# One core, infini-attention with a gated MLP: the prologue, the memory update and the down projection in another order

## The chip, the core and the metric

The kernel runs on one core of a Trainium2 chip. Five engines run their own instruction streams in order and wait for each other through semaphores: TensorE (PE: matmuls and transposes; its weight loads are listed as PEld), VectorE (DVE), ScalarE (ACT), GpSimd (POOL) and SyncE (SP, which here only issues DMAs). The metric is the device time of one execution in microseconds; the lower the better.

## The reference, cut to what matters

One transformer block on x of 2048 x 448 (16 heads of 28), whose two halves are modulated by a vector c. `silu(c) @ w_mod` gives six vectors of 448 (sa, ca, ga, sb, cb, gb).

```
h = layernorm(x) * (1 + ca) + sa
x = x + ga * attention(h)            # 4 segments of 512 rows
h = layernorm(x) * (1 + cb) + sb
x = x + gb * ((sigmoid(h @ w_gate) * (h @ w_up)) @ w_down)
```

In the attention each segment s has a causal softmax of its own (512 x 512 per head). From the second segment on its output is mixed, per head by sigmoid(beta), with a memory read phi(q) @ M / (phi(q) @ z + 1e-6), where M and z sum phi(k)^T v and phi(k) over the segments before. phi(t) is t + 1 for t > 0 and exp(t) below.

## The kernel before, in words

Everything stays on chip: x is loaded as 16 tiles of 128 rows, four to a segment, and the weights are loaded once.

**Steps of a segment s.** `ln1(s)` (L201) normalises four tiles with `ln_tile` (L179): statistics on DVE (`st` L182, `mv` L183), then on POOL the variance plus epsilon (`ve` L185) and its power -0.5 (`rs` L187), then the normalised tile `xn` on DVE (L189). `proj_jobs(s)` transposes them on PE in four chunks (`lntr` L195), which DVE scales into `hT` (L196); then come, for four head groups hc of four heads each, the q and k projections (`pq` L220, cast by ACT into `qT` and by DVE into `kT`), and four v projections (`pv` L231, cast by ACT into `vt`). `mem_jobs(s)` makes phi(k): PE transposes kT (`ptk` L243), ACT takes exp (`ek` L245, two buffers), POOL clips it (L246), DVE adds (`pk` L247); then PE makes the memory's update (`dM` L257), which DVE adds into M and POOL masks into `rm`. Per head group there are three `logits` calls g = 0, 1, 2 (`lg` L290, one PSUM tile of four banks, exp by ACT L293, causal mask by POOL L296), `pv` (`acc` L309 and, for s > 0, the memory read `mem` L316, normalised by DVE and added by POOL into `ou` L343) and `otr` (L351, transposed output to `oT`). `wo_jobs(s)` projects, adds x and runs the second layernorm of each tile on its own (`wo_tile` L354 to L364). `h2_jobs(s)` transposes again, `gu_jobs(s)` makes 14 gate and up tiles (`gps` L373, tanh by ACT L375, `ups` L378, product by DVE into `fT` L381), `down_jobs(s)` four tiles of 14 matmuls each (`dps` L386, residual by DVE L390, stored by SP).

**Modulation.** `mod_cols` (L156) makes sa, ca, sb and cb as columns; `prep_b1` folds ga into w_o on POOL (L438, 4 products) and `prep_b3` folds gb into w_down on POOL (L447, 14 products).

**Order.** PE runs in the order of the calls (`manual_schedule`); for the other engines and queues the framework's scheduler sets the order. PSUM has four one-bank tiles for everything but the logits; a tile is given out when an earlier one's reader is done. The main loop (L469 to L495) calls `logits` for each s, hc and g and between them takes jobs from a list `fill` until a quota of nanoseconds, estimated in the code, is used up. w_q and w_k come in through a staging area in `wd_sb` and are spread by ACT (L101) and POOL (L102). w_down is loaded there later.

## Time and profile before

| | |
|---|---|
| median of 3 runs | 350.73 us (349.46 to 351.97) |
| the profiled execution | 349.13 us |
| its span, first to last instruction | 347.4 us |
| mean granted TensorE clock | 0.916 of full speed |
| busy share of the span | PE 80%, DVE 49%, ACT 41%, POOL 34% |

The span and the chain of waits belong to one profiled execution, which was 1.6 us under the median. In the profile a busy time is the sum of an engine's instructions. The idle time before an instruction is put down to what released it. The granted clock is given as a share of 2.4 GHz, so 0.50 is 1.2 GHz. In the timeline, rows are runs of like instructions: start, time from the first start to the last end, engine, line, operation, output and input, count, and in brackets the idle time before.

### The profile page before, as it was taken

The page shows a single profiled execution, that of the slowest core. Times are in us where ns is not written, and L with a number is a line of the kernel's source. Part 1 is how long each engine was busy: PE and PEld are TensorE (multiplying, and loading weights), DVE is VectorE, ACT ScalarE, POOL GpSimd, SP SyncE. Part 2 cuts the span into 40 slices and gives each one's busy share as a digit, 9 for nine tenths or more (in the row PEclk, how much of TensorE's full clock was granted, in tenths as well). Part 3 has the DMA queues.
Part 4 walks back from the last instruction along what each step waited for, and adds up shares of the span by engine and source line. Part 5 has one row for each costly group of instructions (what it writes and reads, how often), then busy time and mean ns, then how long its engine had stood idle before and what let it go on. Part 6 is the DMA issues. An engine that isn't in the chain of part 4 may idle for free.

```text
span 347.4 us, 5518 instructions
## 1 busy us (share of the span) xinstructions
PE 277.8 (80%) x2232; PEld 144.5 (42%) x2232; DVE 171.0 (49%) x382; ACT 142.0 (41%) x169; POOL 119.3 (34%) x209
## 2 busy tenths in 40 slices
...
GB/s 179 296 288 308 69 2 0 47 48 0 2 2 0 0 2 0 3 0 2 28 26 0 2 0 2 0 29 27 2 1 2 0 2 32 23 1 0 2 13 40
DMA packets 12473, 12.85 MB, mean 37 GB/s; under 512 B 1184, under 2 KB 11552, under 8 KB 12448
## 3 DMA queue, kind: packets, MB, share of 16 engines
...
## 4 chain that ended last, share of the span: by engine, by line
PE 61%; POOL 16%; DVE 10%; ACT 7%; DMA 3%; issue 2%; SPq 0%; POOLq 0%; ACTq 0%
PE gps L373 13%; PE dps L386 12%; PE ups L378 11%; PE pq L220 7%; PE acc L309 4%; POOL wd_sb L447 4%; POOL pT L296 3%; POOL rs L187 3%; PE lg L290 3%; ACT pT L293 3%; DMA wd_sb<-in_A_wq_dram 3%; PE lntr L195 2%; POOL ou L343 2%; DVE st L182 2%; DVE xn L189 2%; PE pv L231 2%
## 5 line engine op out<-in xcount | busy, mean ns | idle before, releaser
L293 ACT ACTIVATE pT<-lg 128x2048 bf16<-128x2048 f32 (+1 forms) x48 | 76.5, 1594 | 50.6 <-PE lg L290 48.2
L296 POOL TENSOR_SCALAR_AFFINE_SELECT pT<-pT 128x512 bf16<-128x512 bf16 x64 | 40.5, 646 | 100.8 <-ACT pT L293 100.7
L375 ACT ACTIVATE tt<-gps 128x512 f32<-128x512 f32 x56 | 33.3, 596 | 88.2 <-PE gps L373 86.8
L381 DVE SCALAR_TENSOR_TENSOR fT<-tt,ups 128x512 bf16<-128x512 f32 x56 | 38.5, 688 | 61.6 <-PE ups L378 36.9
L373 PE MATMUL gps<-hT,wg_sb 112*128 112x512 bf16 x224 | 60.5, 392 | 0.9 <-DVE hT L196 0.8
L378 PE MATMUL ups<-hT,wu_sb 112*128 112x512 bf16 x224 | 58.6, 385 | 0.0
L386 PE MATMUL dps<-wd_sb,fT 128*128 128x448 bf16 x224 | 43.9, 353 | 0.0
L195 PE MATMUL lntr<-ident,xn 128*112 128x128 bf16 x128 | 17.1, 299 | 23.0 <-DVE xn L189 22.3
L378 PEld LDWEIGHTS <-wu_sb 112*128 112x128 bf16 x224 | 22.2, 99 | 27.7 <-issue 2.2
L373 PEld LDWEIGHTS <-wg_sb 112*128 112x128 bf16 x224 | 20.2, 101 | 23.9 <-issue 6.3
L386 PEld LDWEIGHTS <-fT 128*128 128x128 bf16 x224 | 21.4, 98 | 19.7 <-issue 0.5
L195 PEld LDWEIGHTS <-xn 128*112 128x112 bf16 x128 | 13.5, 192 | 27.2 <-DVE xn L189 24.8
L390 DVE TENSOR_TENSOR ot<-dps,x_sb 128x448 bf16<-128x448 f32 x16 | 10.0, 624 | 28.0 <-PE dps L386 28.0
L220 PE MATMUL pq<-hT,wq_sb 112*128 112x512 bf16 x64 | 19.6, 422 | 2.8 <-DVE hT L196 2.6
L257 PE MATMUL dM<-vt,pk 128*128 128x116 bf16 x48 | 6.7, 293 | 18.8 <-DVE pk L247 18.8
L182 DVE BATCH_NORM_STATS2 st<-x_sb 128x6 f32<-128x448 bf16 x32 | 18.7, 608 | 5.1 <-DMA x_sb<-in_A_x_dram 4.9
L189 DVE TENSOR_SCALAR xn<-x_sb,mv,rs 128x448 bf16<-128x448 bf16 x32 | 13.3, 431 | 15.2 <-POOL rs L187 15.0
L309 PEld LDWEIGHTS <-pT 128*128 128x128 bf16 x640 | 18.7, 98 | 2.7 <-issue 0.4
L309 PE MATMUL acc<-vt,pT 128*128 128x29 bf16 x640 | 19.0, 178 | 0.0
L187 POOL TENSOR_TENSOR rs<-ve,mhalf 128x1 f32<-128x1 f32 x32 | 18.0, 569 | 1.7
L290 PE MATMUL lg<-qT,kT 28*128 28x512 bf16 (+3 forms) x256 | 17.7, 309 | 0.8 <-DVE kT L225 0.8
L220 PE MATMUL pq<-hT,wk_sb 112*128 112x512 bf16 x64 | 18.2, 410 | 0.0
...
## 6 DMA issues: line engine op xcount, KB each, us to landing
...
```

The lines of the kernel that those rows point to most:

```text
L187: nc.gpsimd.tensor_tensor(rs[:], ve[:], mhalf[:], ALU.pow)
L195: nc.tensor.transpose(pt[0:KP, t * P:(t + 1) * P], xns[t][:, kc * KP:(kc + 1) * KP], ident[:])
L220: nc.tensor.matmul(pq[:, 0:L], lhsT=head_cols(w_sb, k, hc), rhs=h[:, k, :], start=(k == 0), stop=(k == NK - 1))
L290: nc.tensor.matmul(lg[:, hs, wid:wid + nq], lhsT=kT[r, hc, kb * P:(kb + 1) * P], rhs=qT[r, hc, kb * P:L], start=True, stop=True, tile_posi ...
L293: nc.scalar.activation(pT[:, :, w0:w0 + wid], lg[:, :, 0:wid], AF.Exp, scale=scale)
L296: nc.gpsimd.affine_select(out=blk, in_=blk, compare_op=ALU.is_ge, fill=0.0, base=0, pattern=[[0, 4], [1, P]], channel_multiplier=-1)
L309: nc.tensor.matmul(accv[:, qb, hs, 0:ME], lhsT=pT[:, hs, c0:c0 + P], rhs=vt[:, kb, hc * 4 + hs, 0:ME], start=(kb == 0), stop=(kb == qb))
L373: nc.tensor.matmul(gp[:, 0:L], lhsT=wg_sb[:, k, fs], rhs=h[:, k, :], start=(k == 0), stop=(k == NK - 1))
L375: nc.scalar.activation(tt[:], gp[:, 0:L], AF.Tanh, scale=0.5)
L378: nc.tensor.matmul(up[:, 0:L], lhsT=wu_sb[:, k, fs], rhs=h[:, k, :], start=(k == 0), stop=(k == NK - 1))
L381: nc.vector.scalar_tensor_tensor(ft[:], tt[:], 1.0, up[:, 0:L], op0=ALU.add, op1=ALU.mult)
L386: nc.tensor.matmul(dp[:, 0:D], lhsT=fT_of[(s, fc)][:, t * P:(t + 1) * P], rhs=wd_sb[:, fc, :], start=(fc == 0), stop=(fc == NFC - 1))
```

## The change

Nothing is computed differently but for one thing: the power -0.5 of the first layernorm is taken for the four tiles of a segment in one POOL operation of 128 x 4 instead of four of 128 x 1. The second layernorm still goes tile by tile. All else is order:

- The first layernorm of segment 0 is emitted ahead of the spreading of w_q and w_k. The masks `bmask`, the gate `coef` and the ones in `vt` come after the first projections, in `late_consts`. Most loads come in `late_loads`, in another order.
- The four `mem_k` steps and the `dM` step stand between pieces of the next segment's projections instead of in a row. For segment 2 they stand inside segment 3's projections, behind `prep_b3`.
- In the main loop `pv` stands before `logits` of g = 1, each g has one quota instead of two halves, segments 1 to 3 share one quota that is worked out once, and the down projection of segment s-2 and the second layernorm's transposes are only put into `fill` after `wo_jobs(s-1)`, so the down projection stands between `wo_jobs` and those transposes.
- The tail has other limits: the quota leaves the time of six gate and up tiles unspent, and half of the down projection of segment 2 stands behind the last `wo_jobs`.

```diff
--- before.py
+++ after.py
@@ -89,52 +89,44 @@
     wm = {0: load_wm(nc.sync, 0), 1: load_wm(nc.scalar, 1)}
...
-    for k in range(NK):
-        nc.scalar.copy(wq_sb[:, k, :, 0:Dh], wq_st[:, k, :, :])
-        nc.gpsimd.tensor_copy(wk_sb[:, k, :, 0:Dh], wk_st[:, k, :, :])
     nc.sync.dma_start(wv_sb[:], A_wv.rearrange("(k p) n -> p k n", p=KP))
-    beta_t = const.tile([P, H], BF16)
-    nc.sync.dma_start(beta_t[:], A_beta.partition_broadcast(P))
-    for s in range(1, NSEG):
-        load_x(nc.sync, s * TPS, (s + 1) * TPS)
-    wm[2] = load_wm(nc.sync, 2)
-    wo_sb = wts.tile([KP, NK, D], BF16)
-    nc.sync.dma_start(wo_sb[:], A_wo.rearrange("(k p) n -> p k n", p=KP))
-    wm[3] = load_wm(nc.sync, 3)
-    wm[4] = load_wm(nc.sync, 4)
-    wg_sb = wts.tile([KP, NK, F], BF16)
-    wu_sb = wts.tile([KP, NK, F], BF16)
-    for w_sb, w_dram in ((wg_sb, B_w_gate), (wu_sb, B_w_up)):
-        wv_ = w_dram.rearrange("(k p) n -> p k n", p=KP)
-        nc.sync.dma_start(w_sb[:, 0:2, :], wv_[:, 0:2, :])
-        nc.sync.dma_start(w_sb[:, 2:4, :], wv_[:, 2:4, :])
-    wm[5] = load_wm(nc.sync, 5)
-    nc.sync.dma_start(wd_sb[:], B_w_down.rearrange("(fc p) n -> p fc n", p=P))
+
+    def late_loads():
+        load_x(nc.sync, TPS, 2 * TPS)
+        nc.sync.dma_start(beta_t[:], A_beta.partition_broadcast(P))
+        wm[2] = load_wm(nc.sync, 2)
+        load_x(nc.sync, 2 * TPS, 3 * TPS)
+        nc.sync.dma_start(wo_sb[:], A_wo.rearrange("(k p) n -> p k n", p=KP))
+        wm[3] = load_wm(nc.sync, 3)
+        load_x(nc.sync, 3 * TPS, 4 * TPS)
+        for w_sb, w_dram in ((wg_sb, B_w_gate), (wu_sb, B_w_up)):
+            wv_ = w_dram.rearrange("(k p) n -> p k n", p=KP)
+            nc.sync.dma_start(w_sb[:, 0:2, :], wv_[:, 0:2, :])
+            nc.sync.dma_start(w_sb[:, 2:4, :], wv_[:, 2:4, :])
+        wm[4] = load_wm(nc.sync, 4)
+        nc.sync.dma_start(wd_sb[:], B_w_down.rearrange("(fc p) n -> p fc n", p=P))
+        wm[5] = load_wm(nc.sync, 5)
 
 
...
-    mhalf = const.tile([P, 1], F32)
+    mhalf = const.tile([P, TPS], F32)
     nc.gpsimd.memset(mhalf[:], -0.5)
-
     bmask = const.tile([P, NHC, 4, ME], BF16)
...
-    nc.scalar.activation(coef[:, 1, :], beta_t[:], AF.Tanh, scale=0.5)
-    nc.vector.tensor_scalar(coef[:, 1, :], coef[:, 1, :], 0.5, 0.5, op0=ALU.mult, op1=ALU.add)
-    nc.vector.tensor_scalar(coef[:, 0, :], coef[:, 1, :], -1.0, 1.0, op0=ALU.mult, op1=ALU.add)
-
     vt_all = [const.tile([P, TPS, H, HP], BF16, name=f"vt{s}") for s in range(NSEG)]
-    for s in range(NSEG):
-        nc.gpsimd.memset(vt_all[s][:, :, :, Dh:Dh + 1], 1.0)
+    def late_consts():
+        for s in range(NSEG):
+            nc.gpsimd.memset(vt_all[s][:, :, :, Dh:Dh + 1], 1.0)
+        nc.scalar.activation(coef[:, 1, :], beta_t[:], AF.Tanh, scale=0.5)
+        nc.vector.tensor_scalar(coef[:, 1, :], coef[:, 1, :], 0.5, 0.5, op0=ALU.mult, op1=ALU.add)
+        nc.vector.tensor_scalar(coef[:, 0, :], coef[:, 1, :], -1.0, 1.0, op0=ALU.mult, op1=ALU.add)
+
+        nc.gpsimd.memset(bmask[:], 1.0)
...
 
     def mod_cols(j, vi, plus_one):
         cp = m_f32("cp")
@@ -176,18 +176,21 @@
         return rep
 
 
-    def ln_tile(src):
-        st = work.tile([P, nc.vector.BN_STATS_DIM], F32, tag="st", bufs=4)
-        mv = work.tile([P, nc.vector.BN_AGGR_DIM], F32, tag="mv", bufs=4)
-        nc.vector.bn_stats(st[:], src)
-        nc.vector.bn_aggr(mv[:], st[:])
-        ve = work.tile([P, 1], F32, tag="ve", bufs=4)
-        nc.gpsimd.tensor_scalar(ve[:], mv[:, 1:2], EPS, None, op0=ALU.add)
-        rs = work.tile([P, 1], F32, tag="rs", bufs=4)
-        nc.gpsimd.tensor_tensor(rs[:], ve[:], mhalf[:], ALU.pow)
-        xn = work.tile([P, D], BF16, tag="xn", bufs=8, name="xn")
-        nc.vector.tensor_scalar(xn[:], src, mv[:, 0:1], rs[:, 0:1], op0=ALU.subtract, op1=ALU.mult)
-        return xn
+    def ln_tiles(srcs, key):
+        n = len(srcs)
+        mv = work.tile([P, n, nc.vector.BN_AGGR_DIM], F32, tag=f"mv{n}", bufs=3)
+        for i, src in enumerate(srcs):
+            st = work.tile([P, nc.vector.BN_STATS_DIM], F32, tag="st", bufs=4)
+            nc.vector.bn_stats(st[:], src)
+            nc.vector.bn_aggr(mv[:, i, :], st[:])
+        rs = work.tile([P, n], F32, tag=f"rs{n}", bufs=3)
+        nc.gpsimd.tensor_scalar(rs[:], mv[:, :, 1], EPS, None, op0=ALU.add)
+        nc.gpsimd.tensor_tensor(rs[:], rs[:], mhalf[:, 0:n], ALU.pow)
+        out = xns_of.setdefault(key, [])
+        for i, src in enumerate(srcs):
+            xn = work.tile([P, D], BF16, tag="xn", bufs=8, name="xn")
+            nc.vector.tensor_scalar(xn[:], src, mv[:, i, 0:1], rs[:, i:i + 1], op0=ALU.subtract, op1=ALU.mult)
+            out.append(xn)
 
     def h_chunk(xns, hT, kc, vi):
         pt = m_bf16("lntr")
@@ -199,7 +202,7 @@
     xns_of, hT_of = {}, {}
 
     def ln1(s):
-        xns_of[s] = [ln_tile(x_sb[:, s * TPS + t, :]) for t in range(TPS)]
+        ln_tiles([x_sb[:, s * TPS + t, :] for t in range(TPS)], s)
 
     def new_hT(key):
         hT_of[key] = pipe.tile([KP, NK, L], BF16, tag="hT", bufs=3, name="hT")
@@ -359,9 +362,7 @@
                              start=(k == 0), stop=(k == NK - 1))
         xt = x_sb[:, s * TPS + t, :]
         nc.vector.tensor_tensor(xt, pw[:, 0:D], xt, ALU.add)
-        if t == 0:
-            xns_of[("2", s)] = []
-        xns_of[("2", s)].append(ln_tile(xt))
+        ln_tiles([xt], ("2", s))
 
     fT_of = {}
 
@@ -448,64 +449,72 @@
 
 
     ln1(0)
+    for k in range(NK):
+        nc.scalar.copy(wq_sb[:, k, :, 0:Dh], wq_st[:, k, :, :])
+        nc.gpsimd.tensor_copy(wk_sb[:, k, :, 0:Dh], wk_st[:, k, :, :])
     mod_cols(0, 0, False)
     mod_cols(1, 1, True)
-    ln1(1)
+    late_loads()
     j0 = proj_jobs(0)
     for _, fn in j0[:7]:
         fn()
+    late_consts()
+    ln1(1)
+    j1, j2, j3 = proj_jobs(1), proj_jobs(2), proj_jobs(3)
+    m = [mem_jobs(s) for s in range(3)]
     fill.extend(j0[7:])
-    fill.extend(mem_jobs(0))
-    fill.extend(proj_jobs(1))
+    fill.extend(j1[:5] + m[0][0:2] + j1[5:7] + m[0][2:4] + j1[7:9] + m[0][4:] + j1[9:])
+    fill.append((0, lambda: ln1(2)))
     fill.append((1000, prep_b1))
-    fill.extend(mem_jobs(1))
-    fill.append((0, lambda: ln1(2)))
+    fill.extend(j2[:5] + m[1][0:2] + j2[5:7] + m[1][2:4] + j2[7:9])
     fill.append((2000, prep_b2))
-    fill.extend(proj_jobs(2))
     fill.append((0, lambda: ln1(3)))
+    fill.extend(m[1][4:] + j2[9:])
     fill.append((1000, prep_b3))
-    p3 = proj_jobs(3)
+    rest = j3[:5] + m[2][0:2] + j3[5:7] + m[2][2:4] + j3[7:9] + m[2][4:] + j3[9:]
+
+    def cost(jobs):
+        return sum(cst for cst, _ in jobs)
+
+    quota0 = cost(fill) / 12.0
+    tail_cover = 6 * 8 * MM
+    total = cost(rest) + sum(cost(wo_jobs(s) + h2_jobs(s) + gu_jobs(s)) for s in range(3)) \
+        + sum(cost(down_jobs(s)) for s in range(2)) - tail_cover
+    quota1 = total / 36.0
 
     for s in range(NSEG):
+        quota = quota0 if s == 0 else quota1
         if s == 1:
-            fill.extend(p3)
-            fill.extend(mem_jobs(2))
-        if s >= 2:
-            fill.extend(down_jobs(s - 2))
-        if s >= 1:
-            late = h2_jobs(s - 1) + gu_jobs(s - 1)
-        else:
-            late = []
-        total = sum(cst for cst, _ in list(fill) + late) + (wo_jobs(0)[0][0] * 4 if s else 0)
-        quota = total / 12.0
+            fill.extend(rest)
         debt = 0.0
         for hc in range(NHC):
+            prev = (s, hc - 1) if hc else (s - 1, NHC - 1)
             for g in range(3):
-                logits(s, hc, g)
-                prev = (s, hc - 1) if hc else (s - 1, NHC - 1)
-                debt = run_fill(quota / 2 + debt)
                 if prev[0] >= 0 and g == 1:
                     pv(*prev)
+                logits(s, hc, g)
+                debt = run_fill(quota + debt)
                 if prev[0] >= 0 and g == 2:
                     otr(*prev)
-                    if prev[1] == NHC - 1:
-                        fill.extendleft(reversed(wo_jobs(prev[0])))
-                        fill.extend(late)
-                debt = run_fill(quota / 2 + debt)
-        run_fill(1e9 if s == 0 else 0)
+                    if hc == 0:
+                        fill.extendleft(reversed(wo_jobs(s - 1)))
+                        if s >= 2:
+                            fill.extend(down_jobs(s - 2))
+                        fill.extend(h2_jobs(s - 1) + gu_jobs(s - 1))
+        if s == 0:
+            run_fill(1e9)
     last = NSEG - 1
     fill.extend(down_jobs(last - 1))
-    run_fill(3000)
+    run_fill(2000)
     pv(last, NHC - 1)
-    run_fill(3000)
+    run_fill(6000)
     otr(last, NHC - 1)
-    run_fill(2000)
+    run_fill(500)
     for _, fn in wo_jobs(last):
         fn()
     run_fill(1e9)
     for _, fn in h2_jobs(last) + gu_jobs(last) + down_jobs(last):
         fn()
-
```

**POOL in the prologue.** Names are tiles; `wk_sb<-wd_sb` is the spreading of w_k out of the staging area, `rs` the power -0.5. Before:

```order
L102 COPY wk_sb<-wd_sb 112x16x28 x4
L133 AFFINE_SELECT bmask<-bmask 128x4x29 x3
L135 AFFINE_SELECT bmask<-bmask 128x4x29 x3
L133 AFFINE_SELECT bmask<-bmask 128x4x29
L154 MEMSET vt_151 128x64
L154 MEMSET vt_152 128x64
L135 AFFINE_SELECT bmask<-bmask 128x4x29
L154 MEMSET vt_153 128x64
L154 MEMSET vt_154 128x64
L185 TENSOR_SCALAR ve<-mv 128x1 x4
L187 TENSOR_TENSOR rs<-ve,mhalf 128x1 x4
```

The same stretch now:

```order
L187 TENSOR_SCALAR rs<-mv 128x4
L454 COPY wk_sb<-wd_sb 112x16x28
L188 TENSOR_TENSOR rs<-rs,mhalf 128x4
L454 COPY wk_sb<-wd_sb 112x16x28 x3
L143 MEMSET vt_115 128x64
L143 MEMSET vt_116 128x64
L148 MEMSET bmask 128x464
L150 AFFINE_SELECT bmask<-bmask 128x4x29 x3
L152 AFFINE_SELECT bmask<-bmask 128x4x29 x3
```

The power of segment 0 has moved ahead of three of the four copies of w_k and of all masks.

**POOL around the product of gb and w_down** (`wd_sb<-wd_sb,gb`; `ek` is the clip of phi(k) of segment 2, `pT` a causal mask, `rs` the second layernorm). Before:

```order
L296 AFFINE_SELECT pT<-pT 128x4x128 x5
L447 TENSOR_TENSOR wd_sb<-wd_sb,gb 128x448 x14
L296 AFFINE_SELECT pT<-pT 128x4x128 x4
L185 TENSOR_SCALAR ve<-mv 128x1
L187 TENSOR_TENSOR rs<-ve,mhalf 128x1
```

Now:

```order
L299 AFFINE_SELECT pT<-pT 128x4x128 x4
L448 TENSOR_TENSOR wd_sb<-wd_sb,gb 128x448 x14
L299 AFFINE_SELECT pT<-pT 128x4x128
L249 TENSOR_SCALAR ek<-ek 128x512 x2
L299 AFFINE_SELECT pT<-pT 128x4x128 x2
L249 TENSOR_SCALAR ek<-ek 128x512 x2
```

The clips of segment 2's phi(k) have moved from behind the second layernorm of segment 0 to right behind the 14 products.

**DVE and ACT where segment 1 gives over to segment 2** (`x_sb<-pwo` is the residual of the output projection, `ot<-dps` that of the down projection). DVE before, the end of the second layernorm:

```order
L189 TENSOR_SCALAR xn<-x_sb,mv,rs 128x448
L183 BN_AGGR mv<-st 128x2
L182 BN_STATS st<-x_sb 128x6
L189 TENSOR_SCALAR xn<-x_sb,mv,rs 128x448
L183 BN_AGGR mv<-st 128x2
L189 TENSOR_SCALAR xn<-x_sb,mv,rs 128x448
L196 TENSOR_SCALAR hT<-lntr,cols 112x512 x4
```

DVE now:

```order
L185 BN_AGGR mv<-st 128x2
L391 TENSOR_TENSOR ot<-dps,x_sb 128x448
L192 TENSOR_SCALAR xn<-x_sb,mv,rs 128x448
L391 TENSOR_TENSOR ot<-dps,x_sb 128x448 x2
L325 RECIPROCAL r_2119<-acc 128x16
```

ACT now, a little ahead of it (`pT<-lg` of 4x512, 4x256 and 4x512 are g = 1 and g = 2 of segment 1's last head group and g = 0 of segment 2's first):

```order
L376 ACTIVATE tt<-gps 128x512 x2
L281 ACTIVATE eq<-qT_120 128x512
L296 ACTIVATE pT<-lg 128x4x512
L296 ACTIVATE pT<-lg 128x4x256
L296 ACTIVATE pT<-lg 128x4x512
L281 ACTIVATE eq<-qT_118 128x512
```

On DVE the down projection's residuals now stand inside and behind the second layernorm, ahead of the scaling into `hT`; on ACT three exps follow each other with no gate tile between.

## Rows read from the trace of the kernel before

**Rows 1.** The profile's page: each engine's busy us (share of the span), instructions.
```profile
PE 277.8 (80%) x2232; PEld 144.5 (42%) x2232; DVE 171.0 (49%) x382; ACT 142.0 (41%) x169; POOL 119.3 (34%) x209
```
**Rows 2.** By stretch: start:end, length, busy us (count) PE PEld DVE ACT POOL, PEclk, DMA.
```profile
36.70:93.00 56.30, 44.73 (x414) 26.69 (x412) 22.78 (x46) 30.26 (x40) 21.63 (x32) 0.79 0.06 16
93.00:128.00 35.00, 24.42 (x246) 14.10 (x246) 19.51 (x43) 15.84 (x19) 24.26 (x34) 0.85 0.00 1
128.00:344.10 216.10, 190.00 (x1464) 93.86 (x1463) 106.63 (x233) 84.47 (x94) 54.07 (x85) 0.94 0.03 9
```
**Rows 3.** PE's waits over the span: us in total, times, longest us.
```profile
PE lntr L195 <- DVE xn L189: 22.3, 13, 4.7
PE dM L257 <- DVE pk L247: 18.8, 12, 5.3
...
PE otr L351 <- POOL ou L343: 7.7, 7, 1.1
```
**Rows 4.** Timeline of the prologue.
```profile
13.20 0.16 DVE L163 TENSOR_SCALAR cols<-cp 112x4 f32<-112x4 f32 x1 [1.33 <-PE cp L160]
...
15.98 2.25 POOL L187 TENSOR_TENSOR rs<-ve,mhalf 128x1 f32<-128x1 f32 x4
...
17.45 1.29 DVE L189 TENSOR_SCALAR xn<-x_sb,mv,rs 128x448 bf16<-128x448 bf16 x4
...
17.88 2.55 PE L195 MATMUL lntr<-ident,xn 128*112 128x128 bf16 x16 [4.71 <-DVE xn L189]
...
24.85 1.91 PE L220 MATMUL pq<-hT,wk_sb 112*128 112x512 bf16 x4
...
26.80 0.69 DVE L225 CAST kT<-pq 128x512 bf16<-128x512 f32 x1 [0.73 <-PE pq L220]
```
**Rows 5.** Timeline: a tile of the second layernorm that runs beside a POOL mask (184.35 to 185.61).
```profile
184.42 0.70 DVE L189 TENSOR_SCALAR xn<-x_sb,mv,rs 128x448 bf16<-128x448 bf16 x1 [0.48 <-POOL rs L187]
```
**Rows 6.** Timeline of POOL and PE around the product of gb and w_down.
```profile
93.36 1.10 PE L195 MATMUL lntr<-ident,xn 128*112 128x128 bf16 x16
...
93.83 13.89 POOL L447 TENSOR_TENSOR wd_sb<-wd_sb,gb 128x448 bf16<-128x448 bf16 x14 [1.35 <-ACT gb L175]
...
96.00 1.02 PE L220 MATMUL pq<-hT,wk_sb 112*128 112x512 bf16 x4
...
99.89 1.16 PE L309 MATMUL acc<-vt,pT 128*128 128x29 bf16 x40
```
**Rows 7.** Groups of instructions in 93 to 128 us: busy us, mean ns, idle before.
```profile
L296 POOL TENSOR_SCALAR_AFFINE_SELECT pT<-pT 128x512 bf16<-128x512 bf16 x7 | 4.3, 640 | 0.0
...
L247 DVE SCALAR_TENSOR_TENSOR pk<-ptk,ek 128x512 bf16<-128x512 bf16 x4 | 2.6, 686 | 2.0 <-POOL ek L246 2.0
...
L246 POOL TENSOR_SCALAR ek<-ek 128x512 bf16<-128x512 bf16 x4 | 2.4, 612 | 1.0 <-ACT ek L245 0.9
L245 ACT ACTIVATE ek<-ptk 128x512 bf16<-128x512 bf16 x4 | 2.3, 596 | 5.3 <-DVE pk L247 4.9 <-PE ptk L243 0.4
```
**Rows 8.** Timeline of the last second layernorm.
```profile
284.30 5.46 PE L386 MATMUL dps<-wd_sb,fT 128*128 128x448 bf16 x28
...
297.32 2.63 PE L358 MATMUL pwo<-wo_sb,oT 112*128 112x448 bf16 x13 [0.26 <-DVE oT L352]
...
306.56 1.63 PE L195 MATMUL lntr<-ident,xn 128*112 128x128 bf16 x13 [1.13 <-DVE xn L189]
```
**Rows 9.** The chain of waits behind it: start us, us, what.
```profile
308.19 1.71 PE gps L373 x4
...
311.00 0.86 PE gps L373 x4
```
**Rows 10.** Timeline of one head group of segment 1, and an exp of the next.
```profile
143.07 0.37 PE L316 MATMUL mem<-rm,pqt 128*128 128x116 bf16 x4
...
148.32 0.43 PE L351 MATMUL otr<-ident,ou 128*112 128x128 bf16 x4 [1.10 <-POOL ou L343]
...
154.75 1.88 ACT L293 ACTIVATE pT<-lg 128x2048 bf16<-128x2048 f32 x1 [0.61 <-PE lg L290]
```

19 lines of the change are left out of this document (11 added, 8 removed).

## The prediction

> **What bounds the kernel now.** I read busy time by engine first: PE is busy for 80% of the span and no other engine for half of it [rows 1]. So PE sets the time, and what counts is when it stands still and at which clock it runs. The second view is the table by stretch [rows 2]. It cuts the run in four, of which it shows the last three. Up to 36.7 us (A) lie loads, the first layernorm and segment 0's projections. Up to 93.0 (B) come segment 0's attention and the projections of segments 1 and 2. Up to 128.0 (C) the product of gb and w_down keeps POOL busy while segment 3 is projected. Up to 344.1 (D) it is all MLP and attention. PE's busy time falls short of the length by 11.6, 10.6 and 26.1 us in B, C and D. The reader should also see the clock there: 0.79, 0.85 and 0.94 of full speed.
>
> The third view, PE's waits, names the gaps [rows 3]. Transposes wait 22.3 us for normalised tiles. Of that, 4.7 is the first layernorm. The other 17.6 lie at the second layernorms that end segments 1, 2 and 3, nearly 6 each. `dM` waits 18.8 us for phi(k), and the transposed attention output 7.7 us for POOL. All three kinds are addressed by the change.
>
> **A, the prologue.** The last thing that xn needs in the new order is the column copy that ends at 13.20 + 0.16 = 13.36 [rows 4], since the power is now made on POOL behind one copy of w_k only. Its price at 128 x 4 is not in the trace: at least that of one 128 x 1, 0.57 us, at most four of them, 2.25; by either it is over by 13.4. So xn starts at 13.4 instead of 17.45. Its four tiles take 1.29, to 14.7. The transposes finished 1.7 after the fourth tile before (17.45 + 1.29 to 17.88 + 2.55), so now at 16.4. Before, DVE put tiles of segment 1 ahead of the scaling into hT; now one statistics operation stands there. I put the four hT at half a microsecond each, so 17.3, the last matmul of q's first tile at 17.8, and the four of k take 1.91 as before: 19.7 against 26.8 for the cast of kT [rows 4]. **A gives 7.1.** The least is 4.1, the shift of xn alone; the most 8, if TensorE leaves the lower clock sooner. The loads of x come later in the queue, and a late one would hold DVE ahead of hT; this lies between these ends. The copies of w_q and w_k, which move behind the layernorm, start when their data land, as before.
>
> One rule speaks against this part. A tile of xn took 0.70 us beside a POOL mask [rows 5], but four beside the powers, which POOL was making from 15.98 to 18.23, took 1.29, so 0.32 each [rows 4], and I take that. The Trainium skill (SBUF — State Buffer, SBUF: two separate sides) says that VectorE and GpSimd hold a shared pair of ports as an exclusive lock for a whole instruction; POOL is busy beside the new xn with copies and masks, and by 0.70 each the sum would be 1.5 us worse. The 0.70 agrees with that rule, the 1.29 does not need it.
>
> **B, the memory update between projections.** Before, four transposes were followed at once by `dM`, which waited for the exp, clip and sum; nearly all of the 11.6 us that PE stands in B are this [rows 2, 3]. Now eight projection matmuls and more lie between the pairs. One pair needs two exps, one clip more and one sum: 2 x 0.60 + 0.61 + 0.69 = 2.5 us [rows 7], and eight projection matmuls take, at 0.86 for four of this width, 1.7 [rows 9]. So most is hidden. What remains I put at 4.3 in all: the second pair waits for the two exp buffers, and hT of segment 1 queues behind layernorm statistics on DVE. The four products for w_o on POOL, 1 us each as those for w_down [rows 6], delay the clips of segment 1 by 1.5 of this. The clock gives something back: 0.79 means half speed for 42% of 56.3 us, 23.6 us, of which 11.6 were the waits; 12 us of work at half speed cost up to 6, and I take 4.2 because the small matmuls do not gain in full. **B gives 11.6 + 4.2 - 4.3 = 11.5**; ends 6 (half of the waits stay, no clock) and 14.
>
> **C, the product of gb and w_down.** Here the change adds a wait. The 14 products hold POOL for 13.89 us [rows 6], and the clips of segment 2's phi(k) now stand right behind them. PE has only this to do in that time: output transposes, logits, 16 transposes (1.1), eight of phi(k) (0.5), eight projection matmuls (1.8), `acc` (1.1), logits, eight transposes (0.5). That makes about 6.5 us, and 7.5 with the casts it waits for [rows 6, 9]. The next projection tile needs the PSUM tile of the first phi(k) transposes, which DVE frees only after the clip. That is 0.7 + 13.89 + 0.64 + 0.61 + 0.69 = 16.5 us after gb's matmuls [rows 6, 7]. So PE stands for 9 us. Then the second pair must pass ACT, POOL and DVE (two masks are ahead of it on POOL) before `dM`: some 2 us more. I take PE to be at the lower clock by then, as C's 0.85 shows of its stops [rows 2], for 1.6 more, and I put 0.9 on the layernorm after it. That is 13.5 of idle and slow time instead of 10.6. **C costs 2.9.** Ends: nothing, if the idle time only changes place, and 8, if masks and the layernorm behind them pile up on POOL.
>
> **D, the second layernorms.** Now the output projection is followed by 42, 28 and 28 matmuls of the down projection, and in the first two cases by a head group's work, before the transposes. 28 take 5.4 us [rows 8]. The last layernorm took from the end of the output projection, 299.95, to the transposes at 306.56 [rows 8], so 6.6 us. At the ends of segments 1 and 2 more than 8 us cover it; in the tail 5.4 cover 6.6, and the down projection's residuals stand on DVE ahead of the last tile, so I leave 1.5 there. That is 17.6 - 1.5 = 16.1. The clock: 13 transposes took 1.63 where 16 take 1.10, and the first gate tile 1.71 against 0.86 [rows 6, 8, 9], so 0.7 + 0.9 = 1.6 at each end, 4.8 in all; I take 4.0, since the new gaps below cost some clock too.
>
> The 7.7 us for POOL's `ou` go, since twice as much work stands between `pv` and `otr`: from `mem` to `otr` it took 5.2 us [rows 10], now covered by three gate and up tiles (5.2). In their place come two new gaps. At the end of segment 1 the list runs dry: g = 1 and g = 2 follow each other with no gate work, so PE waits for an exp of 1.88 [rows 10] and then for `ou`. Of the 5.2 and the output copy some 4.3 are left bare. At the end of segment 2 one gate and up tile is left, so 2.3. **D gives 16.1 + 4.0 + 7.7 - 6.6 = 21.2**; ends 13 (clock stays, the tail gets half a cover) and 26.
>
> **Nothing** comes from the later `bmask`, `coef` and `vt`: they are needed 20 us later, and POOL is idle for two thirds of the run [rows 1]. If that cover were gone, `dM` of segment 0 would wait for nine mask operations, at the most 0.64 each [rows 7]. The second layernorm still takes its powers one by one, so the batching is worth nothing there.
>
> **Sum.** 7.1 + 11.5 - 2.9 + 21.2 = 36.9. The profiled execution took 349.13, 1.6 under the median of 350.73. 349.13 - 36.9 = 312.2; on the footing of the median **314 us**.
>
> **The rivals.**
> - *POOL becomes the bound (20%).* For it: the order on POOL puts clips, masks and powers behind the 14 products, and ACT and DVE run in order behind them. Against: POOL is busy for 34% only. C then costs 8, B gives 7 instead of 11.5 and D 16: 349.1 - (7.1 + 7 - 8 + 16) = 327, so 328.
> - *The clock stays up and the gap in C costs nothing (14%).* The 9 us replace waits of the same size, and with no other long stop TensorE keeps 2.4 GHz. C 0, D 25, B 13, A 8: 303, so 305.
> - *The cover does not work (5%).* The last tiles of xn stand behind `ot` on DVE, which waits for the down projection, so the transposes still wait near 6 us three times. D gives 5 instead of 21.2: 330.
> - *Slower (3%).* `pv` now comes ahead of logits g = 1, so it needs the mask of the head group before sooner. If every one of the 11 later head groups stops as at the end of segment 1, 4.3 us, the loss of 47 outweighs the rest from 3.4 us a group on: 349.1 - 36.9 + 47 = 359, so 361. Against it: ACT is busy for 84 of 216 us in D and POOL for 54 [rows 2].
> - Forecast, 58%; its own range is 307 to 321.
>
> Both neighbours lie largely inside 302 to 330, which leaves out about 2 in 10. A change of 1%, 3.5 us, is about what can be told from none. Faster by more than that: 0.95; the same: 0.02; slower: 0.03.
>
> **What would show it.** In the new profile: the first kT cast near 19.7; no wait of `dM` over 2 us before the product of gb; one PE gap of about 9 us behind that product, for phi(k); transposes of the second layernorm without waits at the ends of segments 1 and 2, and about 1.5 in the tail; gaps of about 4 and 2 before the output projections of segments 1 and 2; mean clock over 0.95. I am wrong if PE's waits outside A sum to more than 30 us, or if the gap in C exceeds 14.

## The result, and the profile after

The changed kernel takes 316.36 us in the median (316.01 to 321.37, 4 runs) where the kernel before took 350.1 (349.07 to 351.97): a ratio of 0.9026, 95% interval 0.8983 to 0.9069. A second set of runs gave 0.9042 (0.8958 to 0.9126). The forecast was 314, its range 302 to 330. The profiled execution of the change took 321.37 us, 5.0 more than the median, and nearly all of that is TensorE's clock in B, the second of the four stretches below (0.85; 0.96 in the execution with idle matmuls further down, which is the same up to 74 us), so for B that one is quoted too; why the clock there differs between executions is open.

The page of the change, which answers to [rows 1]:

```profile
PE 274.4 (86%) x2232; PEld 144.8 (45%) x2232; DVE 170.2 (53%) x382; ACT 140.5 (44%) x169; POOL 113.4 (35%) x185
```

PE is busy for only 1.2% less, so in this execution what went is nearly all standing time: 347.4 - 277.8 = 69.6 us before, 319.6 - 274.4 = 45.2 now. With B from the other execution PE's busy time is 5.0 us lower again; that part of the gain is the clock, not standing time. The table by stretch of the change, cut at the same events as [rows 2] (end of segment 0's value projections, end of gb's matmuls, first gate tile, last matmul), with the columns of [rows 2]:

```profile
33.80:78.80 45.00, 42.75 (x413) 25.89 (x410) 22.98 (x48) 29.53 (x39) 23.15 (x33) 0.85 0.18 50
78.80:123.10 44.30, 28.70 (x253) 14.78 (x251) 20.94 (x44) 17.05 (x20) 25.45 (x35) 0.77 0.00 1
123.10:316.30 193.20, 184.59 (x1462) 93.79 (x1459) 104.56 (x232) 81.97 (x94) 52.34 (x84) 0.98 0.03 10
```

The same B in the kernel with idle matmuls in C:

```profile
34.10:74.10 40.00, 37.71 (x411) 22.77 (x410) 22.78 (x48) 29.54 (x39) 22.97 (x33) 0.96 0.20 56
```

| us | before | predicted gain | after | measured gain |
|---|---|---|---|---|
| A | 36.7 | 7.1 | 33.8 | 2.9 |
| B | 56.3 | 11.5 | 40.0 | 16.3 |
| C | 35.0 | -2.9 | 44.3 | -9.3 |
| D | 216.1 | 21.2 | 193.2 | 22.9 |
| sum | | 36.9 | | 32.8 |

The sum came out 4 us short, but two stages are off by 4 to 6 us in one direction and one by 5 in the other. The total is thus better than its parts. PE's waits in the change answer to [rows 3]:

```profile
PE pq L223 <- DVE pk L250: 8.9, 2, 8.7
PE lg L293 <- ACT pT L296: 6.6, 5, 3.9
PE pv L234 <- DVE t L339: 3.6, 1, 3.6
PE lntr L198 <- DVE xn L192: 2.9, 2, 1.8
PE pv L234 <- DVE kT L228: 2.7, 1, 2.7
PE ptk L246 <- DVE ou L336: 1.8, 2, 1.5
PE dM L260 <- DVE pk L250: 1.6, 2, 1.3
```

Transposes wait 2.9 us for normalised tiles instead of 22.3, `dM` 1.6 instead of 18.8, and `otr` no longer appears. New are the 8.7 us of a projection tile for phi(k), foreseen as 9, the 3.9 of logits for an exp at the end of segment 1, foreseen as part of 4.3, and two long ones that were not foreseen: 3.6 us of a value projection for DVE's `t` (line 339, `t1` in the code) and 2.7 for a cast of kT.

The prologue's timeline answers to [rows 4] (start, length, engine, line, operation; in brackets the idle time before and its releaser):

```profile
11.29 1.05 POOL L188 TENSOR_TENSOR rs<-rs,mhalf 128x4 f32<-128x4 f32 x1
...
13.35 2.62 DVE L192 TENSOR_SCALAR xn<-x_sb,mv,rs 128x448 bf16<-128x448 bf16 x4
...
15.02 2.64 PE L198 MATMUL lntr<-ident,xn 128*112 128x128 bf16 x16 [1.78 <-DVE xn L192]
...
20.70 0.69 DVE L228 CAST kT<-pq 128x512 bf16<-128x512 f32 x1 [1.02 <-PE pq L223]
...
32.91 0.92 PE L234 MATMUL pv<-wv_sb,hT 112*128 112x448 bf16 x4 [2.75 <-DVE kT L228]
```

xn starts at 13.35 as forecast, but its four tiles take twice the 1.29 us. The first kT cast comes 6.1 us earlier than before, not 7.1. Then 2.75 us are lost at 30.2, where PE waits for the cast of the last kT tile. DVE shows why: four more tiles of a layernorm, for a segment that is not due yet, stand ahead of that cast, and they wait for POOL:

```profile
29.73 1.94 DVE L192 TENSOR_SCALAR xn<-x_sb,mv,rs 128x448 bf16<-128x448 bf16 x4 [0.97 <-POOL rs L188]
31.58 0.17 DVE L185 BATCH_NORM_AGGREGATE mv<-st 128x2 f32<-128x6 f32 x1
31.68 0.59 DVE L184 BATCH_NORM_STATS2 st<-x_sb 128x6 f32<-128x448 bf16 x1
32.19 0.67 DVE L228 CAST kT<-pq 128x512 bf16<-128x512 f32 x1
```

C in the change, POOL and then PE, answers to [rows 6]:

```profile
93.31 0.65 POOL L299 TENSOR_SCALAR_AFFINE_SELECT pT<-pT 128x512 bf16<-128x512 bf16 x1
93.91 1.21 POOL L249 TENSOR_SCALAR ek<-ek 128x512 bf16<-128x512 bf16 x2
...
95.32 1.86 PE L223 MATMUL pq<-hT,wq_sb 112*128 112x512 bf16 x4 [8.71 <-DVE pk L250]
96.98 1.84 PE L223 MATMUL pq<-hT,wk_sb 112*128 112x512 bf16 x4
...
106.10 1.03 PE L223 MATMUL pq<-hT,wk_sb 112*128 112x512 bf16 x4
...
116.91 1.30 PE L234 MATMUL pv<-wv_sb,hT 112*128 112x448 bf16 x3 [3.62 <-DVE t L339]
```

POOL ends the product at 93.3, makes a mask and the two clips, and PE runs again at 95.3. The projections behind the gap take 1.86 us where the same four matmuls take 1.03 at 106. And the tail's layernorm, which answers to [rows 8]:

```profile
272.88 5.46 PE L387 MATMUL dps<-wd_sb,fT 128*128 128x448 bf16 x28
278.18 0.33 PE L198 MATMUL lntr<-ident,xn 128*112 128x128 bf16 x3
279.66 0.93 PE L198 MATMUL lntr<-ident,xn 128*112 128x128 bf16 x13 [1.16 <-DVE xn L192]
```

It now waits 1.16 us behind 5.46 us of the down projection; 1.5 had been put there. The transposes take 0.93 instead of 1.63, so the clock was kept.

### The profile page after: what moved, and what is told of

It is laid out like the page before. It is cut to its first block, busy times and chain, and to the rows that moved or that the text cites. A ratio compares the mean times of both kernels' runs of the same rounds, so it can differ in the third digit from the quotient of the medians.

```text
span 319.6 us, 5477 instructions
## 1 busy us (share of the span) xinstructions
PE 274.4 (86%) x2232; PEld 144.8 (45%) x2232; DVE 170.2 (53%) x382; ACT 140.5 (44%) x169; POOL 113.4 (35%) x185
## 3 DMA queue, kind: packets, MB, share of 16 engines
q10 hardware_dynamic: 1200, 1.03, 1.2%
## 4 chain that ended last, share of the span: by engine, by line
PE 70%; DVE 11%; POOL 9%; ACT 4%; DMA 3%; issue 1%; SPq 0%; POOLq 0%; ACTq 0%
PE gps L374 15%; PE ups L379 15%; PE dps L387 11%; PE pq L223 9%; POOL wd_sb L448 4%; PE acc L312 4%; PE lg L293 4%; PE pwo L361 3%; PE pv L234 3%; ACT pT L296 3%; DMA wm<-in_w_mod_dram 3%; DVE xn L192 2%; PE cp L160 2%; DVE st L184 2%; PE lntr L198 2%; POOL rs L188 2%
## 5 line engine op out<-in xcount | busy, mean ns | idle before, releaser
L299 POOL TENSOR_SCALAR_AFFINE_SELECT pT<-pT 128x512 bf16<-128x512 bf16 x64 | 40.1, 642 | 58.6 <-ACT pT L296 58.6
L374 PE MATMUL gps<-hT,wg_sb 112*128 112x512 bf16 x224 | 59.2, 380 | 0.7
L379 PE MATMUL ups<-hT,wu_sb 112*128 112x512 bf16 x224 | 57.5, 379 | 0.0
L346 POOL TENSOR_TENSOR ou<-t,t 128x448 bf16<-128x448 f32 x12 | 13.6, 1134 | 25.9 <-DVE t L345 25.9
L234 PE MATMUL pv<-wv_sb,hT 112*128 112x448 bf16 x64 | 16.0, 395 | 6.4 <-DVE t L339 3.6
L184 DVE BATCH_NORM_STATS2 st<-x_sb 128x6 f32<-128x448 bf16 x32 | 18.8, 607 | 5.0 <-DMA x_sb<-in_A_x_dram 4.9
L223 PE MATMUL pq<-hT,wk_sb 112*128 112x512 bf16 x64 | 20.1, 445 | 0.0
L192 DVE TENSOR_SCALAR xn<-x_sb,mv,rs 128x448 bf16<-128x448 bf16 x32 | 14.3, 470 | 10.1 <-POOL rs L188 10.1
L187 POOL TENSOR_SCALAR rs<-mv 128x1 f32<-128x1 f32 (+1 forms) x20 | 4.8, 239 | 41.1 <-DVE mv L185 34.2
L281 ACT ACTIVATE eq<-qT 128x512 bf16<-128x512 bf16 x12 | 7.6, 632 | 26.7 <-DVE pqt L284 26.6
L228 DVE CAST kT<-pq 128x512 bf16<-128x512 f32 x16 | 11.0, 685 | 14.8 <-PE pq L223 14.8
(73 smaller groups left out, 316.4 us busy)
## 6 DMA issues: line engine op xcount, KB each, us to landing
wg_sb<-in_B_w_gate_dram SPq DMA_DIRECT2D x2, 784.0 KB, 11.6
wd_sb<-in_B_w_down_dram SPq DMA_DIRECT2D x1, 1568.0 KB, 21.2
```

The lines of the kernel that those rows point to most:

```text
L184: nc.vector.bn_stats(st[:], src)
L223: nc.tensor.matmul(pq[:, 0:L], lhsT=head_cols(w_sb, k, hc), rhs=h[:, k, :], start=(k == 0), stop=(k == NK - 1))
L234: nc.tensor.matmul(pv[:, 0:D], lhsT=h[:, k, t * P:(t + 1) * P], rhs=wv_sb[:, k, :], start=(k == 0), stop=(k == NK - 1))
L299: nc.gpsimd.affine_select(out=blk, in_=blk, compare_op=ALU.is_ge, fill=0.0, base=0, pattern=[[0, 4], [1, P]], channel_multiplier=-1)
L374: nc.tensor.matmul(gp[:, 0:L], lhsT=wg_sb[:, k, fs], rhs=h[:, k, :], start=(k == 0), stop=(k == NK - 1))
L379: nc.tensor.matmul(up[:, 0:L], lhsT=wu_sb[:, k, fs], rhs=h[:, k, :], start=(k == 0), stop=(k == NK - 1))
```

## The experiments

Each kernel is the changed one with one edit. A ratio is to the kernel before on the same chip; a difference in us is (ratio - 0.9026) x 350.1, and the change's own interval is 1.5 us to either side. Stage times are those of one profiled execution. Against the change's A 33.8, B 40.0, C 44.3 and D 193.2 they read:

| | ratio (95%) | us | A | B | C | D |
|---|---|---|---|---|---|---|
| prologue back | 0.9185 (0.9123 to 0.9248) | +5.6 | 37.1 | 42.9 | 43.5 | 192.9 |
| memory updates in a row | 0.9391 (0.9336 to 0.9445) | +12.8 | 34.0 | 52.6 | 44.5 | 193.1 |
| segment loop back | 0.9654 (0.9569 to 0.974) | +22.0 | 33.4 | 42.8 | 40.1 | 216.4 |
| product spread | 0.8886 (0.8809 to 0.8963) | -4.9 | 33.7 | 40.2 | 33.9 | 196.4 |
| segment 2's update last | 0.8735 (0.8697 to 0.8772) | -10.2 | 33.9 | 40.0 | 34.8 | 193.5 |
| constants later | 0.903 (0.8977 to 0.9084) | +0.1 | 34.9 | 39.6 | 43.6 | 193.0 |
| second layernorm batched | 0.9073 (0.9013 to 0.9133) | +1.6 | 34.2 | 40.1 | 44.4 | 194.1 |
| last kT cast on ACT | 0.8971 (0.8947 to 0.8994) | -1.9 | 30.9 | 42.4 | 43.6 | 193.0 |
| idle matmuls in the gap | 0.8923 (0.889 to 0.8955) | -3.6 | 34.1 | 40.0 | 40.0 | 193.1 |
| combined 1 | 0.8724 (0.8693 to 0.8754) | -10.6 | 32.7 | 42.8 | 36.9 | 188.9 |
| combined 2 | 0.8682 (0.865 to 0.8713) | -12.0 | 30.9 | 42.7 | 37.5 | 189.1 |

**The change once more.**

> The changed kernel as it is, for a second look at its trace. Near 316 us. By the trace shown first, PE stops four times outside the prologue's loads for longer than 2 us: 8.7 us behind the product of gb and w_down (a projection tile that waits for phi(k)), 3.6 us where the attention product waits for DVE's t1, 2.75 us where a value projection waits for kT's cast, 3.9 us where logits wait for an exp. Theory 1: all four are set by the order of the program and come again within 1 us each. Rival: those of 3.6 and 2.75 are races that are sometimes lost; then they are gone and the span is some 5 us shorter than 319.6.

All four stops came again, within 0.2 us of the first trace (8.7, 3.6, 2.7 and 3.9 us longest), and every experiment that leaves their place alone has them too. They are set by the order, not by chance; the rival falls.

**Undoing A: the prologue back.**

```diff
-    ln1(0)
     for k in range(NK):
         nc.scalar.copy(wq_sb[:, k, :, 0:Dh], wq_st[:, k, :, :])
         nc.gpsimd.tensor_copy(wk_sb[:, k, :, 0:Dh], wk_st[:, k, :, :])
+    late_loads()
+    late_consts()
+    ln1(0)
     mod_cols(0, 0, False)
     mod_cols(1, 1, True)
-    late_loads()
+    ln1(1)
...
-        ln_tiles([x_sb[:, s * TPS + t, :] for t in range(TPS)], s)
+        for t in range(TPS):
+            ln_tiles([x_sb[:, s * TPS + t, :]], s)
```

> Prologue alone put back: copies of w_q and w_k, late loads, masks and coef ahead of the first layernorm, the layernorm of segment 1 ahead of the projections, powers one tile at a time; all the rest stays as changed. By the prediction's term (A gives 7.1 us) it takes 316.0 + 7.1 = 323 us, bounds 320 to 324. Rival, from the end of segment 0's projections in the changed kernel's trace (33.7 us against 36.9): most of the 7 us is given back in a wait for kT's cast, and the prologue is worth 3.2: 319 us.

Measured +5.6 us, between the two, nearer to the prediction's 7.1; its interval alone reaches from 3.4 to 7.8. The stage table shows how: A is longer by 3.3, B by 2.9.

```profile
37.10:80.00 42.90, 38.63 (x411) 22.52 (x409) 23.78 (x46) 29.66 (x40) 23.02 (x33) 0.96 0.11 29
```

The wait of 2.7 us for kT's cast is gone in this kernel, and in B PE stands still for 4.3 us (42.9 less 38.6 of work) where the change has 2.3. So the prologue is worth more than A shows by itself: what the change loses at the cast it has back in B, where it waits less.

**Undoing B: the memory updates in a row.**

```diff
-    fill.extend(j1[:5] + m[0][0:2] + j1[5:7] + m[0][2:4] + j1[7:9] + m[0][4:] + j1[9:])
+    fill.extend(m[0] + j1)
...
-    fill.extend(j2[:5] + m[1][0:2] + j2[5:7] + m[1][2:4] + j2[7:9])
+    fill.extend(m[1] + j2[:9])
...
-    fill.extend(m[1][4:] + j2[9:])
+    fill.extend(j2[9:])
```

> The memory updates of segments 0 and 1 put back in a row ahead of the next segment's projections; segment 2's stays spread, and so does all the rest. By the prediction's term (B gives 11.5 us: 11.6 of waits and 4.2 of clock against 4.3 of new waits) it takes 316.0 + 11.5 = 327.5 us, bounds 322 to 330, with waits of dM for phi(k) of 5 us and more each, twice, in its trace. Rival: the spread only moves the wait to other places (PSUM tiles, the two exp buffers), so that putting it back costs under 5 us: below 321 us.

Measured +12.8, which is 1.3 over the prediction's 11.5. B of this kernel, and its wait:

```profile
34.00:86.60 52.60, 41.33 (x412) 25.19 (x410) 23.28 (x48) 29.92 (x39) 22.77 (x33) 0.81 0.16 44
```
```profile
PE dM L260 <- DVE pk L250: 12.1, 10, 3.1
```

`dM` waits 12.1 us in all, 1.6 in the change. Of the 12.6 us by which B is longer, PE's standing time makes 9.0 (52.6 - 41.3 against 40.0 - 37.7) and its slower work 3.6 (41.3 against 37.7, clock 0.81 against 0.96). The single waits are 3.1 at the most, not 5: the expectation erred there.

**Undoing D: the loop over segments back.**

```diff
             for g in range(3):
-                if prev[0] >= 0 and g == 1:
-                    pv(*prev)
                 logits(s, hc, g)
-                debt = run_fill(quota + debt)
+                prev = (s, hc - 1) if hc else (s - 1, NHC - 1)
+                debt = run_fill(quota / 2 + debt)
+                if prev[0] >= 0 and g == 1:
+                    pv(*prev)
...
-                    if hc == 0:
+                    if prev[1] == NHC - 1:
-                        fill.extendleft(reversed(wo_jobs(s - 1)))
-                        if s >= 2:
-                            fill.extend(down_jobs(s - 2))
-                        fill.extend(h2_jobs(s - 1) + gu_jobs(s - 1))
+                        fill.extendleft(reversed(wo_jobs(prev[0])))
+                        fill.extend(late)
+                debt = run_fill(quota / 2 + debt)
```

> The loop over segments put back as before: pv behind logits g = 1, half quotas, gate and up jobs and second-layernorm transposes straight behind the output projection, the down projection ahead of the list, the old tail numbers; prologue and spread memory update stay as changed. By the prediction's term (D gives 21.2 us) it takes 316.0 + 21.2 = 337 us, bounds 329 to 342; the transposes of the second layernorm wait about 6 us three times and the transposed attention output 0.8 us in each of 9 head groups. Rival (the second layernorm was hidden by DVE's order anyway, the gain came with the earlier stages): under 326 us.

Measured +22.0, against 21.2. By the stages D is 23.2 us longer and B 2.8, and C is 4.2 shorter. Its waits carry the names that were expected:

```profile
PE lntr L198 <- DVE xn L192: 20.0, 14, 2.3
...
PE otr L354 <- POOL ou L346: 7.7, 7, 1.1
```

The 17.6 us of the second layernorms and the 7.7 of `otr` are back, D is 216.4 as before, and its clock 0.94.

**C, first way: the product out of the clips' way.**

```diff
-    def prep_b3():
-        gb = mod_rep(5, 0.5, "gb")
-        for fc in range(NFC):
-            nc.gpsimd.tensor_tensor(wd_sb[:, fc, :], wd_sb[:, fc, :], gb[:], ALU.mult)
...
+    def gb_block(j):
+        cs = slice(j * CB, (j + 1) * CB)
+        rp = m_f32("rp")
+        for k in range(NK):
+            nc.tensor.matmul(rp[:, 0:CB], lhsT=silu_bc[:, k, :], rhs=wm[5][:, k, cs],
+                             start=(k == 0), stop=(k == NK - 1))
+        nc.scalar.mul(gb[:, cs], rp[:, 0:CB], 0.5)
+        nc.gpsimd.tensor_tensor(wd_sb[:, :, cs], wd_sb[:, :, cs],
+                                gb[:, cs].rearrange("p (o n) -> p o n", o=1).to_broadcast([P, NFC, CB]), ALU.mult)
...
             jobs.append((8 * MM, lambda fc=fc: gate_up(s, fc)))
+            if s == 0 and fc % 2 == 0:
+                jobs.append((0, lambda j=fc // 2: gb_block(j)))
```

> The product of gb and w_down is taken from the front of POOL's queue and made in 7 blocks of 64 columns, each behind its own 4 small matmuls, between the gate and up tiles of segment 0 in stage D; the same products, the same engine. Theory 1 (the clips of segment 2's phi(k) stand behind 14 us of products): the gap of 8.7 us in C goes, the clock in C rises from 0.77 towards 0.95, C shrinks from 44.4 to 30 to 33 us, the added small matmuls cost about 1 us: 303 to 307 us in all. Rival 1 (the gap is the trip of phi(k) through ACT, POOL and DVE with two exp buffers, and POOL's queue is only the last to be named): a gap of over 4 us stays and the time is over 311. Rival 2 (the 2 us blocks hold up the masks of segment 1 in D): C shrinks as said but D grows by as much, 314 to 317.

The gap is gone: no wait of `pq` over 0.3 us is left. So it was POOL's queue. C and D of this kernel:

```profile
73.90:107.80 33.90, 27.73 (x245) 14.85 (x243) 19.71 (x43) 16.12 (x19) 11.70 (x22) 0.80 0.00 1
107.80:304.20 196.40, 187.00 (x1491) 94.72 (x1488) 104.91 (x233) 83.15 (x100) 65.08 (x91) 0.97 0.03 10
```

C lost 10.4 us, 8.7 of them the gap. But its clock rose only to 0.80. The projections still run at half speed, and now the only stops of PE just ahead of them are three waits of `dM`, 0.8, 1.3 and 0.4 us:

```profile
83.42 0.23 PE L260 MATMUL dM<-vt,pk 128*128 128x116 bf16 x1 [1.26 <-DVE pk L250]
...
85.72 1.89 PE L223 MATMUL pq<-hT,wq_sb 112*128 112x512 bf16 x4
87.40 1.91 PE L223 MATMUL pq<-hT,wk_sb 112*128 112x512 bf16 x4
```

D grew by 3.2, of which 2.4 are more PE work (28 added matmuls among it). 311 is not the 303 to 307 of theory 1: it was right about the gap and wrong about the clock. Of rival 1 no gap of over 4 us stayed, and of rival 2 D grew by a third of what C lost.

**C, second way: segment 2's update back behind segment 3's projections.**

```diff
-    rest = j3[:5] + m[2][0:2] + j3[5:7] + m[2][2:4] + j3[7:9] + m[2][4:] + j3[9:]
+    rest = j3 + m[2]
```

> Only segment 2's memory update goes back to its old place, in a row behind segment 3's projections; the product stays in front on POOL. By the prediction's term (C costs 2.9 us) it takes 316 - 2.9 = 313 us. By the two traces (C 44.4 us against 34.9 before) it takes 316 - 9.5 = 306.5 us, with the gap of 8.7 us gone and dM waiting some 6 to 8 us for phi(k) instead. Rival (C is long for another reason, the layernorm behind the output projection): 316 within 1 us.

One line, and 10.2 us faster. The prediction's term of 2.9 is refuted; the 9.5 of the traces stands. C is what it was before the change:

```profile
73.90:108.70 34.80, 25.58 (x253) 15.01 (x251) 20.47 (x45) 17.23 (x20) 25.79 (x36) 0.86 0.00 1
```

`dM` waits only 2.3 us, not the 6 to 8 that were expected; the transposes ahead of it wait 3.4 and 1.1 us for DVE's `t1` and `t2` (lines 339 and 345) instead. The 3.6 us stop has only changed its victim. It goes with the new segment loop: in the kernel with the loop back, the wait for `t1` in C is 1.2 us.

**C's clock: idle matmuls in the gap.** This kernel adds 36 matmuls whose result nobody reads; the rest is complete.

```diff
+    def keep_warm():
+        lg = ps_lg.tile([P, 4, 512], F32, tag="lg", name="warm")
+        for i in range(36):
+            nc.tensor.matmul(lg[:, i % 4, :], lhsT=ident[:], rhs=wd_st(i), start=True, stop=True)
+
+    def wd_st(i):
+        return kT_of[2][:, i % 4, :]
...
-    rest = j3[:5] + m[2][0:2] + j3[5:7] + m[2][2:4] + j3[7:9] + m[2][4:] + j3[9:]
+    rest = j3[:5] + m[2][0:2] + j3[5:7] + m[2][2:4] + [(0, keep_warm)] + j3[7:9] + m[2][4:] + j3[9:]
```

> 36 idle matmuls of 128 x 512 (7.8 us at full clock, their result is not used) stand in the gap of 8.7 us behind the product of gb and w_down; all the rest as changed. Theory 1 (4 us of C's loss is the lower clock after that gap: the projections behind it take 1.9 us where 1.03 is the time at full clock): the projections behind the gap take 1.03 us, PE's own work in C falls by 3 to 4 us and the run takes 312 to 313 us. Rival 1 (the clock behind the gap falls for the shorter waits that follow it, for dM and t1): 315 to 316 us. Rival 2 (the idle matmuls run past the end of the gap, or take PSUM or queue room from others): 317 us and more.

Measured -3.6, as theory 1 has it. PE's timeline there, and behind it the row of C:

```profile
82.45 8.99 PE L454 MATMUL warm<-kT,ident 128*128 128x512 bf16 x34 [0.22 <-issue]
91.28 1.03 PE L223 MATMUL pq<-hT,wq_sb 112*128 112x512 bf16 x4
92.14 1.03 PE L223 MATMUL pq<-hT,wk_sb 112*128 112x512 bf16 x4
...
108.04 1.93 PE L234 MATMUL pv<-wv_sb,hT 112*128 112x448 bf16 x8 [3.62 <-DVE t L339]
```
```profile
74.10:114.10 40.00, 33.79 (x288) 18.07 (x288) 21.58 (x45) 16.99 (x20) 25.98 (x36) 0.90 0.00 1
```

The matmuls fill the 8.7 us, and the projections behind them take 1.03 instead of 1.86. C shrinks from 44.3 to 40.0. Without the idle matmuls (0.41 + 8.99 us) PE's own work in C is 33.8 - 9.4 = 24.4 us, where the change has 28.7; what is left, standing time and idle matmuls together, is 15.6 us in both. So 4.3 us of C were the granted clock, 0.77 against 0.90; by the other traces that leave C alone, where PE works 27.9 to 28.4 us in it, 3.5 to 4.0. The gap is not its only possible cause, though: with the product spread the gap is gone and PE's work in C is still 27.7 us. There `dM` waits for 2.4 us; in the change it waits for 1.6, and in this kernel, whose PE is busy through the gap, for only 0.3. So half speed came with either stop and without the other: in the change the slow matmuls begin ahead of the waits of `dM`, and in the kernel with the product spread there is no gap. The idle matmuls took both stops away.

**The 3.6 us stop: the second layernorm batched.**

```diff
-        ln_tiles([xt], ("2", s))
+        if s == NSEG - 1:
+            ln_tiles([xt], ("2", s))
+        elif t == TPS - 1:
+            ln_tiles([x_sb[:, s * TPS + i, :] for i in range(TPS)], ("2", s))
```

> The second layernorm of segments 0 to 2 is taken for four tiles at once, with one power of 128 x 4 in place of four of 128 x 1; the last segment keeps single tiles. Theory 1 (the 3.6 us stop of the attention product comes from DVE, where three tiles of the second layernorm wait for POOL's powers one by one ahead of t1): the stop goes and the time is 312 to 313 us. Rival (the four tiles now finish later, so the transposes of the second layernorm wait instead): the same time as the change within 1 us, with a wait of lntr of 3 us or more where none was.

The rival: +1.6 us, with an interval that overlaps the change's. The stop of `t1` is gone, and the transposes wait as long:

```profile
116.37 2.55 PE L198 MATMUL lntr<-ident,xn 128*112 128x128 bf16 x16 [3.58 <-DVE xn L192]
```

So theory 1 is right about who holds `t1` and wrong about what that is worth. A likely reason, not tried: between the output projection of segment 0 and its first gate tile PE has not enough other work, since there is no down projection yet such as covers the later ones.

**A, the slow tiles: constants made later.**

```diff
-            nc.gpsimd.memset(vt_all[s][:, :, :, Dh:Dh + 1], 1.0)
+            nc.gpsimd.tensor_scalar(vt_all[s][:, :, :, Dh:Dh + 1], kT_of[0][:, 0, 0:TPS * H].rearrange(
+                "p (t h o) -> p t h o", t=TPS, o=1), 0.0, 1.0, op0=ALU.mult, op1=ALU.add)
...
-        nc.gpsimd.memset(bmask[:], 1.0)
+        nc.gpsimd.tensor_scalar(bmask[:].rearrange("p c h e -> p (c h e)"), kT_of[0][:, 0, 0:NHC * 4 * ME],
+                                0.0, 1.0, op0=ALU.mult, op1=ALU.add)
```

> The ones in vt and the mask of the memory, which POOL makes while DVE normalises the first four tiles, are made from the first cast of kT instead (0 x kT + 1), so POOL is idle beside those four tiles; same number of POOL instructions. Theory 1 (the four tiles take 2.25 to 2.62 us instead of the 1.29 of before because POOL's copies and memsets are beside them): the four take 1.3 to 1.5 us, kT's first cast starts 0.9 us earlier than 20.4 to 20.7, and the run is 0 to 1 us shorter, 315 to 316. Rival (the loads that land in SBUF at that time, or the tiles themselves, make them slow): the four stay at 2.2 to 2.6 us.

```profile
13.67 1.31 DVE L194 TENSOR_SCALAR xn<-x_sb,mv,rs 128x448 bf16<-128x448 bf16 x4
19.19 0.69 DVE L230 CAST kT<-pq 128x512 bf16<-128x512 f32 x1 [0.27 <-PE pq L225]
...
25.27 1.62 DVE L194 TENSOR_SCALAR xn<-x_sb,mv,rs 128x448 bf16<-128x448 bf16 x4 [3.58 <-POOL rs L190]
```

With POOL idle the four tiles take 1.31 us, and the cast is at 19.19, even before the 19.7 that was forecast. Theory 1 holds. The run is not shorter, though: the constants now hold POOL from 20.0 to 24.2 us, DVE waits 3.58 us behind them for the power of segment 1, and PE then waits 2.4 and 1.2 us for later casts of kT. So the edit moves the constants into the way of another layernorm, and its +0.1 us is not the price of the slow tiles alone.

**A, the wait for kT: the last cast on ACT.**

```diff
-            jobs.append((4 * MM, lambda hc=hc: proj_qk(s, hc, wk_sb, kT_of[s], "dve")))
+            jobs.append((4 * MM, lambda hc=hc: proj_qk(s, hc, wk_sb, kT_of[s],
+                                                       "act" if (s, hc) == (0, NHC - 1) else "dve")))
```

> The cast of segment 0's last kT tile goes from DVE to ACT; nothing else moves by hand. Theory 1 (DVE, busy with the layernorms of segments 1 and 2, holds that cast and with it a PSUM tile, and PE's value projections wait 2.75 us): the wait goes, A ends near 31 us instead of 33.7, the run takes 313 to 314 us. Rival (what is won there is lost again in B, where hT of segment 1 waits for the same DVE): 315.5 to 316.5 us, with a new wait for hT or another cast of 2 us or more.

A is 2.9 us shorter and B 2.4 longer: the next thing that waits for DVE is the transposition behind segment 1's hT.

```profile
34.02 1.04 PE L246 MATMUL ptk<-ident,kT 128*128 128x128 bf16 x8 [2.14 <-DVE hT L199]
```

-1.9 us by the ratio (its interval overlaps that of the change), -0.5 by A and B. In A and B the rival has most of it, while the time, 314.7 us, lies between the two forecasts: DVE is behind here, and moving one wait uncovers the next.

**Two versions for speed.** Both have `rest = j3 + m[2]`, the cast on ACT, and quotas for each segment apart; the first also makes the constants later.

```diff
-    quota1 = total / 36.0
+    seg_work = cost(wo_jobs(0) + h2_jobs(0) + gu_jobs(0))
+    carry = 9100
+    quotas = [quota0, (cost(rest) + seg_work - carry) / 12.0, (seg_work + cost(down_jobs(0))) / 12.0,
+              (carry + seg_work + cost(down_jobs(1)) - tail_cover) / 12.0]
...
-        quota = quota0 if s == 0 else quota1
+        quota = quotas[s]
```

> A version for speed from what the runs show: segment 2's memory update behind segment 3's projections (306.4 us alone), the last kT cast of segment 0 on ACT, vt's ones and the mask made from kT, and quotas for each segment apart, so that each of the segments 1 and 2 leaves 9.1 us of gate and up work for the first head group of the next. Theory: the waits of logits for the exp at the ends of segments 1 and 2 (3.9, 1.2 and 0.5 to 0.6 us) go, worth 6 us with their clock, the first two prologue edits are worth 2 to 3 us: 297 to 300 us. Rival (the waits at the segment ends only move to the masks and exps of segment 1, whose slots get shorter by 0.3 us each): 303 to 306 us.

> As f1_combined, but the ones of vt and the mask are made early on POOL again, as in the change, since the run with that edit alone won nothing (316.2 us) and its A and B together were 74.5 us where the kT cast on ACT alone gave 73.3. By adding stages of earlier runs: A and B 73.3 (kT cast on ACT), C 36.9 and D 188.9 (f1), 3.3 behind: a span of 302.4, some 303 to 304 us, 2 us under f1. Rival (stages don't add, what one gains the next gives back): 305 to 306 us.

The quotas do what they should: D falls from 193.5 to 188.9 and 189.1 with its clock at 1.00, and the waits for the exp at the ends of segments 1 and 2 are gone (one of 1.2 us early in D and two of `otr`, 0.8 each, are new). But C is 2 to 3 us longer than with the one-line edit alone, so the first version gave only 0.4 us over that: its theory of 297 to 300 us failed, and its 305.8 lies in the rival's range. Without the later constants 304.71 us in the median is the lowest here (ratio 0.8682), 12 us under the change; its interval overlaps those of the first version and of the one-line edit. Its C and D:

```profile
73.60:111.10 37.50, 29.41 (x260) 16.25 (x258) 21.04 (x46) 18.07 (x21) 26.02 (x36) 0.79 0.00 1
111.10:300.20 189.10, 182.43 (x1455) 92.19 (x1453) 103.66 (x230) 81.11 (x93) 51.81 (x83) 1.00 0.03 10
```

The stages added up to 302.4 us of span, 303.5 were measured.

C is not longer for its waits: in the second version PE stands for 8.1 us there, and for 9.2 with the one-line edit. Its work is 3.8 us more. Some 1.1 of that is a logits tile and an `otr` (0.61 and 0.63) that now stand ahead of the first gate tile and count to C, where they counted to D; the rest goes with the clock, 0.79 against 0.86. So a part of D's gain is only the cut between the stages.

## Why the prediction was right, and where it was wrong

**The total** (314 against 316.4) was right by mechanisms that the three undone parts confirm in size: prologue 5.6 us against 7.1, memory updates 12.8 against 11.5, segment loop 22.0 against 21.2. That it is off by only 2.4 is in part luck: by the stages A gave 4.2 us less than forecast and C cost 6.4 more, against 4.8 more from B and 1.7 from D. The mean clock, put at over 0.95, was 0.946 to 0.957 in the executions near the median.

**D** was right step by step: the transposes of the second layernorm no longer wait at the ends of segments 1 and 2, 1.16 us are left in the tail (1.5), `otr` is gone, and logits wait 3.9 + 0.5 and 1.2 + 0.6 us where gaps of 4.3 and 2.3 had been put. They were put ahead of the output projection and come one step sooner, at the logits.

**B** was under-sized. The step "what remains I put at 4.3 in all" measured 2.3 (40.0 less 37.7 us of work), and the clock went to 0.96, which is worth more than 4.2: PE's work fell from 44.7 to 37.7. That 7.0 is over the bound of 6, which had laid all 11.6 us of waits into the time at half speed. And 2.9 of B's gain belong to the prologue, as undoing that shows.

**A** failed at "Its four tiles take 1.29, to 14.7", and then at taking the shift of one cast for the gain of the stage. The first: xn took 2.62 us for four tiles, and the cast of kT came at 20.7, not 19.7. The Trainium skill (SBUF — State Buffer, SBUF: two separate sides) says that VectorE and GpSimd hold their shared ports as an exclusive lock. The trace agrees in that the four tiles took 2.25 to 2.62 us with POOL's copies, memsets and masks beside them and 1.31 with POOL idle; the 1.29 beside POOL's powers before does not show such a lock. The prediction had weighed that rule and taken the other row; the 1.5 us that it put on the rule is near the 1.3 that xn took more. The second is DVE's backlog: its layernorms of the next segments hold the last kT cast, which costs 2.75 us in A and comes back in part as a shorter B.

**C** is the step that was wrong. "PE stands for 9 us" (8.7), and "some 2 us more" for `dM` (1.6) were right. "1.6 more" for the clock was 3.5 to 4.3, by the idle matmuls. "0.9 on the layernorm after it" was 3.6, plus 1.5 for `ou` ahead of the second pair of transposes. The 13.5 us of idle and slow time were near 20, so C costs 9.3 (8.5 to 9.5 by the other traces that leave it alone) and not 2.9, beyond the bound of 8. The prediction named the place and the mechanism and under-priced what follows the stop: half speed for the next 10 us of matmuls, and the wait for `t1`. The two edits meet here: with the old loop and the spread update C takes 40.1 us, 5.1 more than before; with the new loop and the update last 34.8, no more than before; with both 44.3.

The rival "POOL becomes the bound" had C nearly right (8) and was wrong on B and D. Its condition, that clips and masks pile up behind the 14 products, held in C alone. The rivals on the cover and on `pv` ahead of the logits are refuted by D, the rival that the gap in C costs nothing by C.

**Left open:** why the clock in C is lower in the second version than with the one-line edit alone, though PE stands less there.
